# Hash-masked attention with a gated MLP: two outputs written in place, one more buffer in two rings, an odd head's copies three tiles earlier, one small product four tiles later

## The chip, the cores and the metric

The kernel runs on one core of one Trainium2 chip. The metric is the device time of one launch, in microseconds (us). Engines are named as the profile names them: PE is TensorE (matrix products; PEld is its loading of weights), DVE is VectorE, ACT is ScalarE, POOL is GpSimd and SP is SyncE, which only issues DMAs here. A "q" behind an engine (SPq, ACTq) means its instruction queue, where DMAs are issued.

## The reference, cut to what matters

Shapes: batch 4, 8 heads, 768 positions, head dimension 64; model width 512, inner width 1024. Each query and key gets a 6-bit bucket from the signs of its projection, and a query attends only to keys of its own bucket. The attention's output feeds a gated MLP whose gate mixes positions.

```python
q_bits = (einsum('bhsd,dk->bhsk', q, proj) > 0); k_bits = ...
mask = q_bucket[:, :, :, None] == k_bucket[:, :, None, :]
scores = where(mask, matmul(q, k^T) / sqrt(64), -1e9)
attn = exp(scores - max(scores)); attn = attn / (sum(attn) + 1e-9)
x = concat_heads(matmul(attn, v))                      # 4 x 768 x 512
h = maximum(x @ w_in, 0); u, v = h[..., :512], h[..., 512:]
v_n = (v - mean(v)) / sqrt(var(v) + 1e-6)
out = (u * (einsum('ts,bsd->btd', w_spatial, v_n) + b_spatial)) @ w_out
```

## The kernel before, in words

There are 32 heads (4 batches of 8), taken in 16 pairs; `p` or `r` is a pair, `n` a head, `i` one of the six tiles of 128 queries of a head, and `g = 6 n + i` counts tiles. Most values are kept as two fp16 numbers, a high part and a residual, so that fp16 products add up to nearly fp32.

Preparation of a pair: `load_qk` fetches q and k (tile `qk`, one buffer); `hash_rows` makes the signed bits (`sg`); `split_qk` (lines 185 to 191) makes high parts and residuals (`hl`, one buffer), the first on ScalarE (line 188). `build(n)` (lines 193 to 212) copies one head's rows from `hl` and `sg` into one of four operand tiles `ab`, with two large DMAs on SyncE's queue and four small ones, which go on ScalarE's queue for heads from 8 on and on SyncE's before. `split_v` prepares v; `mean_v` (lines 221 to 233) adds v up on GpSimd (lines 225 to 228, the last result is `vc`), sums it over partitions with a product on TensorE (line 230) and copies it into `fm` on ScalarE (line 232). `fm` is for queries whose bucket holds no key, and `normalize` reads it after the head's last tile.

A tile of a query head (`scores`, lines 278 to 301): four products give the masked scores in PSUM (lines 291 and 292); VectorE finds the negated row maximum `nb` (line 293), where the elementwise output `jk` is thrown away; ScalarE takes the exponential into `ex` (line 295, three buffers), copies it to fp16 in `pp` (line 298, `PB` = 3 buffers); VectorE or, for some tiles, GpSimd adds the residual (line 299); a DMA on SyncE's queue transposes `pp` into `pt` (line 301, `PTB` = 5 buffers). `weighted` (lines 303 to 316) multiplies `pt` with v, five tiles later (`LAG`). Heads 1 to 7 (`KEYS`) go another way: scores come out transposed (`scores_k`, lines 256 to 266), the maximum is found ahead (`row_max`), no transpose is needed, and the exponentials lie in the `pt` ring.

When the eight heads of a batch are through, its MLP goes into a queue of 28 units, of which one is taken about every 1.7 tiles: six `v_unit`s (line 361 products, line 365 into `v32m`, four buffers, shared with the output `o` of line 435), which after each third call `norm` (lines 374 to 390): line 388 normalizes into `vy`, line 389 copies it to fp16, line 390 makes the residual on GpSimd; then `u_unit`, `s_unit` and `o_unit`. The last batch's units run by themselves after the last head.

Order: each engine carries out its instructions in a fixed order, made by a planner from priorities (`at(g, k)`, in tiles) and from a simulated timeline. The main loop (lines 504 to 569) sets the priorities. Before, head `n` builds head `n + 2` at its tile 0; the mean of the next pair, its product included, is at tile 5 of the even head; in the odd head v is loaded at tile 1, bits are made at tile 2, `split_qk` comes at tile 3 and `load_qk` at tile 5.

Of the kernel before, what the change touches and what calls it, by code (L numbers as in the profile page):

```python
# [10 lines left out]
BF16 = mybir.dt.bfloat16  # L11
F32 = mybir.dt.float32
# [3 lines left out]
ALU = mybir.AluOpType  # L16
# [3 lines left out]
P = 128  # L20
# [16 lines left out]
def lsh_attention_spatial_gating(  # L37
# [11 lines left out]
    nc = tc.nc  # L49
    B, NPAIR, _, _, S = kq.shape  # L50
    NH = 2 * NPAIR
    NT = S // P
    HS = S // 2
    DM = NPAIR * P
    DF = w_in.shape[1]
    F2 = DF // 2
    NF = F2 // P
    ISQ = 1.0 / (SQ * SQ * 8.0)

    VYB = 2  # L60
    QKB = 1
    PSB = (2,2,2)
    MT = "m"
# [2 lines left out]
    wk = ctx.enter_context(tc.tile_pool(name="wk", bufs=1))  # L66
# [35 lines left out]
    st = {}  # L102
# [65 lines left out]
    def has_queries(p):  # L168
        return not (2 * p in KEYS and 2 * p + 1 in KEYS)
# [23 lines left out]
    def build(n):  # L193
        p, e = divmod(n, 2)
        hl, sg, t = st["hl", p], st["sg", p], ab[n % NAB]
        r = slice(D * e, D * e + D)
        q_s, q_h = (BQ_S[n >= NH], BQ_H[n >= NH])
        if n < 1:
            nc.sync.dma_start(out=t[0:D, 2:4], in_=hl[r, 1:3])
        for j in range(4):  # L200
            q_s.dma_start(
                out=t[D:NR, 3 - j // 2, (j % 2) * HS:(j % 2 + 1) * HS],
                in_=sg[32 * j + 16 * e:32 * j + 16 * e + 2 * NB, :])
        if n < 1:
            q_h.dma_start(out=t[0:D, 0:2], in_=hl[r, 0:2])
        else:

            top = hl[r, 0:2]
            (ps, pn), (ss, sn), (es, en) = top.ap
            src = replace(top, ap=[(ps, pn), (ss, 2), (ss, 2), (es, en)])  # L210
            q_h.dma_start(out=t[0:D].rearrange("p (a b) s -> p a b s", b=2), in_=src)
        q_h.dma_start(out=t[D:P, 0:2], in_=hl[r, 2:4])
# [8 lines left out]
    def mean_v(p):  # L221
        v32 = st["v32", p] if has_queries(p) else vf[p % 2][:, :, 0:D]

        a = wk.tile([P, NT, D], F32, tag="pf", name=f"va{p}")
        nc.gpsimd.tensor_add(a, v32[:, 0:NT], v32[:, NT:2 * NT])
        c = wk.tile([P, 2, D], F32, tag="vc", name=f"vc{p}")
        nc.gpsimd.tensor_add(c, a[:, 0:2], a[:, 2:4])
        nc.gpsimd.tensor_add(c, c, a[:, 4:6])
        mp = ps_m.tile([P, 512], F32, tag=MT, name=f"mp{p}")
        nc.tensor.matmul(mp[:, :P], lhsT=ones, rhs=c.rearrange("p e d -> p (e d)"), start=True, stop=True)  # L230
        fm = wk.tile([P, 2, D], F32, tag="fm", bufs=2, name=f"fm{p}")
        nc.scalar.activation(fm.rearrange("p e d -> p (e d)"), mp[:, :P], AF.Copy, scale=SX / S)
        st["fm", p] = fm
# [44 lines left out]
    def scores(n, i):  # L278
        if n in KEYS:
            scores_k(n, i)  # L280
            return
        t = ab[n % NAB]
        if i == 0:
            st["nb", n] = wk.tile([P, NT], F32, tag="nb", bufs=3, name=f"nb{n}")
        nb = st["nb", n][:, i:i + 1]
        jk = wk.tile([P, 2, HS], BF16, tag="jk", name=f"jk{n}_{i}")
        qs = slice(i * P, (i + 1) * P)
        ps = ps_sc.tile([P, 2, 512], F32, tag="sc", name=f"sp{n}_{i}")[:, :, :HS]
        for c in range(2):
            cs = slice(c * HS, (c + 1) * HS)  # L290
            nc.tensor.matmul(ps[:, c], lhsT=t[:, 0, qs], rhs=t[:, 1, cs], start=True, stop=False)  # L291
            nc.tensor.matmul(ps[:, c], lhsT=t[0:P - 1, 3, qs], rhs=t[0:P - 1, 2, cs], start=False, stop=True)  # L292
        nc.vector.tensor_scalar(jk, ps, -ISQ, None, op0=ALU.mult, op1=ALU.min, accum_out=nb)  # L293
        ex = wk.tile([P, 2, HS], F32, tag="ex", bufs=EB, name=f"ex{n}_{i}")
        st["ex", n, i] = nc.scalar.activation(ex, ps, AF.Exp, bias=nb, scale=ISQ).ins  # L295
        at(NT * n + i + G_H, 50)
        pp = wk.tile([P, 2, 2, HS], F16, tag="pp", bufs=PB, name=f"pp{n}_{i}")
        nc.scalar.copy(pp[:, 0], ex)  # L298
        (nc.gpsimd if i in (PL_POOL if n >= 2 * NH else PL_POOL1) else nc.vector).tensor_tensor(out=pp[:, 1], in0=ex, in1=pp[:, 0], op=ALU.subtract)  # L299
        pt = st["pt", n, i] = wk.tile([P, 2 * NT, P], F16, tag="pt", bufs=PTB, name=f"pt{n}_{i}")  # L300
        st["tr"] = nc.sync.dma_start_transpose(out=pt, in_=pp.rearrange("p g c k -> p (g c k)")).ins
# [48 lines left out]
    def mlp_units(b):  # L350
# [3 lines left out]
        v32 = {}  # L354
# [19 lines left out]
        def norm(g):  # L374
            m = mv[g]
            ve = wk.tile([P, 3], F32, tag="ve", bufs=2, name=f"ve{b}_{g}")
            nc.vector.tensor_scalar(ve, m[:, :, 1], EPS_LN, None, op0=ALU.add)
            r = wk.tile([P, 3], F32, tag="rs", bufs=2, name=f"rs{b}_{g}")
            nc.scalar.activation(r, ve, AF.Ln)
            nc.scalar.activation(r, r, AF.Exp, scale=-0.5)  # L380

            nc.vector.tensor_mul(ve, ve, r)
            nc.vector.scalar_tensor_tensor(out=ve, in0=ve, scalar=-0.5 * SN, in1=r, op0=ALU.mult, op1=ALU.mult)
            nc.vector.scalar_tensor_tensor(out=r, in0=ve, scalar=1.5 * SN, in1=r, op0=ALU.add, op1=ALU.mult)
            for j in range(3):
                i = 3 * g + j
                y = wk.tile([P, F2], F32, tag="vy", bufs=VYB, name=f"vy{b}_{i}")
                nc.vector.tensor_scalar(y, v32[i], m[:, j, 0:1], r[:, j:j + 1], op0=ALU.subtract, op1=ALU.mult)
                nc.scalar.copy(vn[0][:, i], y)
                nc.gpsimd.tensor_tensor(out=vn[1][:, i], in0=y, in1=vn[0][:, i], op=ALU.subtract)  # L390

# [55 lines left out]
    N = B * NH  # L447
    NP = B * NPAIR
# [13 lines left out]
        return 99  # L462

    RB = 3
    PB = 3
    EB = 3
    PTB = 5
    XTB = 6
    LAG = 5
    XL_ENG = nc.vector  # L470
# [9 lines left out]
    BQ_S = (nc.sync, nc.scalar)  # L480
    BQ_H = (nc.sync, nc.sync)
    LQ = nc.sync
    BI = 0

    def at(g, k):
        tc.cur_priority = int(1000 * (g + 40) + k)
# [17 lines left out]
    for g in range(N * NT + LAG):  # L504
        n, i = divmod(g, NT)
        if n < N:
            at(g + G_S, 0)
            scores(n, i)
            r = n // 2
            at(g + G_P, 300)  # L510
            if g == 0:
                hash_rows(1)
                split_qk(1)
                split_v(0)
                load_qk(2)
                load_v(1)
                load_vf(0)
                load_vf(1)
            at(g + G_M, 100)
            while rml and rml[0][0] <= g:  # L520
                row_max(*rml.pop(0)[1:])
            at(g + G_P, 300)
            stack = ExitStack()
            if n not in KEYS:
                stack.enter_context(tc.issue_after(st["tr"]))
            if BQ_S[n + 2 >= NH] is nc.scalar or BQ_H[n + 2 >= NH] is nc.scalar:
                stack.enter_context(tc.issue_after(st["ex", n, i]))
            if i == BI and n + 2 < N:
                build(n + 2)
            if n % 2 == 0:  # L530
                if i == 4 and 0 < r < NP - 1:
                    load_vf(r + 1)
                if i == 5 and r + 1 < NP:
                    split_v(r + 1)
                    mean_v(r + 1)
                if i == 4 and r == 0:
                    mean_v(0)
            else:
                if i == 2 and r + 2 < NP:
                    hash_rows(r + 2)  # L540
                if i == 3 and r + 2 < NP:
                    split_qk(r + 2)
                if i == 5 and r + 3 < NP:
                    load_qk(r + 3)
                if i == 1 and r + 2 < NP:
                    load_v(r + 2)
            stack.close()
        while wv < N * NT and wv + (LAGK if wv // NT in KEYS else LAG) <= g:
            m, j = divmod(wv, NT)
            wv += 1  # L550
            at(g + G_V, 200)
            weighted(m, j)
            if j == NT - 1:
                at(g + G_N, 250)
                normalize(m)
                if m % 2:
                    transpose_x(m // 2)
                    if m % NH == NH - 1:
                        queue += mlp_units(m // NH)
        at(g + G_W, 500)  # L560
        while wdone < W_AT(g):
            wdone += 1
            next(wg, None)
        if queue and n < N:
            credit += 28.0 / DEN
            at(g + G_U, 400)
            while queue and credit >= 1.0:
                queue.pop(0)()
                credit -= 1.0
# [44 lines left out]
```

## Time and profile before

| what | before |
|---|---|
| median of three runs | 738.57 us (736.13 to 741.49) |
| profiled execution, span from first to last instruction | 741.7 us |
| TensorE, VectorE, ScalarE, GpSimd busy | 631.5, 520.6, 434.8, 321.2 us |
| share of the 16 DMA engines, SyncE's queue | 76.4% |
| moved in all | 120.95 MB |

The page gives the span of the profiled execution; a time around the span isn't on it, so the span stands beside the runs' own times. A row of waits reads "who waited <- for whom: us in total, times, longest us". A row of a group reads: line, engine, operation, output <- inputs, shapes, count | busy us, mean ns of one | idle us before, and what ended it. A row of the timeline reads: start us, duration us, engine, line, operation, output <- inputs, count, and in brackets the idle time before it and what ended that. Idle time of an engine that isn't the bound costs nothing.

### The profile page before, as it was taken

The numbers are of one execution on the slowest core, as the hardware profiler recorded it, in microseconds if no ns is written. First come the engines' busy times: TensorE is split into PE (matmuls) and PEld (weight loads), VectorE is DVE, ScalarE is ACT, GpSimd is POOL, SyncE is SP. The second block draws the span as 40 slices with busy tenths as digits, with TensorE's granted clock in tenths as the row PEclk, the third lists the DMA queues.
The fourth block names the chain that finished last, engine by engine and source line by source line (L and its number), as shares of the span: only waits on it lengthen the run. The fifth ranks groups of instructions, "written<-read, shape, count | busy, mean of one in ns | idle before, by whom it ended". The sixth has DMA issues, their size and how long they took to land.

```text
span 741.7 us, 14927 instructions
## 1 busy us (share of the span) xinstructions
PE 631.5 (85%) x5759; PEld 400.4 (54%) x5759; DVE 520.6 (70%) x945; ACT 434.8 (59%) x668; POOL 321.2 (43%) x324
## 2 busy tenths in 40 slices
PE   1569898998988776997898899889898998999997
PEld 0237686776445444554544555556455565654553
DVE  4677795536799999567689798678698987755200
ACT  1344574346788676655676577667677776743221
POOL 5122443123458675264314565156235571451503
PEclk9768797999999989898999999999999999999999
DMA  9565554324999989996999799999999999860011
GB/s 235 149 123 155 133 148 102 99 55 97 224 237 197 215 207 187 213 178 138 234 202 199 138 210 213 211 211 212 206 210 181 194 175 213 182 136 15 1 42 43
DMA packets 290011, 120.95 MB, mean 163 GB/s; under 512 B 270740, under 2 KB 273812, under 8 KB 289940
## 3 DMA queue, kind: packets, MB, share of 16 engines
q1 hardware_dynamic: 287636, 119.11, 76.4%
q10 hardware_dynamic: 2304, 0.89, 0.5%
q8 instruction: 45, 0.74, 0.4%
q14 instruction: 26, 0.21, 0.1%
HBM read 28.33 MB, written 6.29 MB: 47 GB/s over the span
## 4 chain that ended last, share of the span: by engine, by line
PE 43%; DMA 21%; DVE 13%; issue 8%; ACT 6%; POOL 6%; SPq 3%; ACTq 0%; DVEq 0%; POOLq 0%
DMA pt<-pp 14%; PE pv L275 6%; PE vps L361 6%; PE ops L432 5%; PE sps L417 5%; PE ups L402 5%; DMA ab<-hl 4%; PE sp L291 3%; DVE jk L293 3%; PE sp L292 3%; DVE pp L299 2%; PE sp L262 2%; PE pv L314 2%; ACT ex L295 2%; PE sp L263 2%
## 5 line engine op out<-in xcount | busy, mean ns | idle before, releaser
L295 ACT ACTIVATE ex<-sp,nb 128x768 f32<-128x768 f32 x150 | 134.1, 897 | 54.8 <-DVE jk L293 48.9
L299 DVE TENSOR_TENSOR pp<-ex,pp 128x768 f16<-128x768 f32 x116 | 126.2, 1089 | 47.6 <-ACT pp L298 46.5
L293 DVE TENSOR_SCALAR_CACHE_REDUCE jk<-sp 128x768 bf16<-128x768 f32 x150 | 142.4, 949 | 24.1 <-PE sp L292 22.2
L298 ACT CAST pp<-ex 128x768 f16<-128x768 f32 x150 | 124.3, 829 | 50.0 <-DMA pt<-pp 43.9
L314 PE MATMUL pv<-vp,pt 128*128 128x65 f16 x900 | 108.2, 198 | 40.5 <-DMA pt<-pp 40.2
L291 PE MATMUL sp<-ab 128*128 128x384 f16 x300 | 103.2, 344 | 31.6 <-ACT ex L295 19.3
L314 PEld LDWEIGHTS <-pt 128*128 128x128 f16 x900 | 86.7, 101 | 67.2 <-DMA pt<-pp 53.4
L299 POOL TENSOR_TENSOR pp<-ex,pp 128x768 f16<-128x768 f32 x34 | 58.1, 1708 | 131.1 <-ACT pp L298 124.6
L315 PE MATMUL pv<-vp,pt 128*128 128x64 f16 x900 | 108.0, 197 | 0.0
L316 PE MATMUL pv<-vp,pt 128*128 128x65 f16 x900 | 107.8, 198 | 0.0
L292 PE MATMUL sp<-ab 127*128 127x384 f16 x300 | 103.9, 346 | 0.0
L417 PE MATMUL sps<-ws,vn 128*128 128x384 f16 x576 | 100.9, 329 | 1.5 <-DVE sg L180 1.0
L315 PEld LDWEIGHTS <-pt 128*128 128x128 f16 x900 | 87.0, 100 | 11.3 <-issue 1.3
L316 PEld LDWEIGHTS <-pt 128*128 128x128 f16 x900 | 86.9, 100 | 3.1 <-issue 0.5
L417 PEld LDWEIGHTS <-vn 128*128 128x128 f16 x576 | 55.3, 99 | 37.8 <-issue 3.9
L432 PE MATMUL ops<-wo,g 128*128 128x512 f16 x288 | 70.9, 391 | 1.5 <-ACT o L436 0.9
L275 PEld LDWEIGHTS pv<-vf,ex 128*128 128x128 f32 x504 | 68.5, 208 | 4.1 <-issue 1.6
L402 PE MATMUL ups<-xt,wi 128*128 128x384 f16 x384 | 69.1, 333 | 1.3 <-ACT u L405 0.9
L361 PE MATMUL vps<-wi,xt 128*128 128x512 f16 x288 | 68.0, 383 | 1.4 <-DMA xt<-xs 1.3
L275 PE MATMUL pv<-vf,ex 128*128 128x65 f32 x504 | 67.0, 286 | 0.0
L333 POOL TENSOR_TENSOR x<-x,xf 128x384 f32<-128x384 f32 x32 | 35.5, 1110 | 64.1 <-DVE x L332 64.1
L422 POOL TENSOR_TENSOR sy<-sy,u 128x384 f32<-128x384 f32 x32 | 36.6, 1145 | 49.3 <-DVE sy L421 49.2
(87 smaller groups left out, 1010.7 us busy)
## 6 DMA issues: line engine op xcount, KB each, us to landing
qk<-kq SPq DMA_DIRECT2D x16, 768.0 KB
ab<-hl SPq DMA_DIRECT2D x31, 384.0 KB
ab<-hl SPq DMA_DIRECT2D x34, 192.0 KB
out<-o SPq DMA_DIRECT2D x24, 256.0 KB
v<-v SPq DMA_DIRECT2D x13, 384.0 KB
raw<-w_in SPq DMA_DIRECT2D x16, 256.0 KB
pt<-pp SPq DMA_TRANSPOSE x150
raw<-w_sp SPq DMA_DIRECT2D x12, 192.0 KB
```

The source lines that it names most:

```text
L275: nc.tensor.matmul(acc[:, qi, :], lhsT=ex[:, qi * P:(qi + 1) * P], rhs=vf[p % 2][:, 2 * i + e, :], start=(i == 0 and qi == 0), stop=(i == ...
L291: nc.tensor.matmul(ps[:, c], lhsT=t[:, 0, qs], rhs=t[:, 1, cs], start=True, stop=False)
L292: nc.tensor.matmul(ps[:, c], lhsT=t[0:P - 1, 3, qs], rhs=t[0:P - 1, 2, cs], start=False, stop=True)
L293: nc.vector.tensor_scalar(jk, ps, -ISQ, None, op0=ALU.mult, op1=ALU.min, accum_out=nb)
L295: st["ex", n, i] = nc.scalar.activation(ex, ps, AF.Exp, bias=nb, scale=ISQ).ins
L298: nc.scalar.copy(pp[:, 0], ex)
L299: (nc.gpsimd if i in (PL_POOL if n >= 2 * NH else PL_POOL1) else nc.vector).tensor_tensor(out=pp[:, 1], in0=ex, in1=pp[:, 0], op=ALU.subtract)
L314: nc.tensor.matmul(acc, lhsT=pt[:, c, :], rhs=vh, start=(i == 0 and c == 0), stop=False)
L315: nc.tensor.matmul(acc[:, 0:D], lhsT=pt[:, c, :], rhs=vl, start=False, stop=False)
L316: nc.tensor.matmul(acc, lhsT=pt[:, NT + c, :], rhs=vh, start=False, stop=(i == NT - 1 and c == NT - 1))
L361: nc.tensor.matmul(ps, lhsT=xt[c][:, gx, i * P:(i + 1) * P], rhs=wi[gw][:, c, F2:DF], start=(k == 0), stop=(k == 3 * NPAIR - 1))
L417: nc.tensor.matmul(ps[:, :HS], lhsT=vn[gv][:, c, d * P:(d + 1) * P], rhs=ws[gw][:, c, hs], start=(k == 0), stop=(k == 3 * NT - 1))
```

## The change

Five things change. The discarded output `jk` is written into the first half of `ex`, as bf16, and `ex` is therefore taken ahead of line 293. The normalized `y` of `norm` is written over its input `v32[i]`, and the buffers `vy` go. `PB` goes from 3 to 4 and `PTB` from 5 to 6. The even head `n` builds both heads of the next pair, `n + 2` at its tile 0 and `n + 3` at its tile 3, where before the odd head built its own successor `n + 2` at tile 0. The product and the copy of `mean_v` become `mean_mm`, called at tile 3 of the odd head, four tiles after `mean_v` (for pair 0 at tile 0 of head 1).

```diff
-    VYB = 2
...
         nc.gpsimd.tensor_add(c, c, a[:, 4:6])
+        st["vc", p] = c
+
+    def mean_mm(p):
+        c = st.pop(("vc", p))
         mp = ps_m.tile([P, 512], F32, tag=MT, name=f"mp{p}")
         nc.tensor.matmul(mp[:, :P], lhsT=ones, rhs=c.rearrange("p e d -> p (e d)"), start=True, stop=True)
...
-        jk = wk.tile([P, 2, HS], BF16, tag="jk", name=f"jk{n}_{i}")
+        ex = wk.tile([P, 2, HS], F32, tag="ex", bufs=EB, name=f"ex{n}_{i}")
+        jk = ex.rearrange("p c k -> p (c k)").bitcast(BF16)[:, 0:S].rearrange("p (c k) -> p c k", c=2)
...
         nc.vector.tensor_scalar(jk, ps, -ISQ, None, op0=ALU.mult, op1=ALU.min, accum_out=nb)
-        ex = wk.tile([P, 2, HS], F32, tag="ex", bufs=EB, name=f"ex{n}_{i}")
...
-                y = wk.tile([P, F2], F32, tag="vy", bufs=VYB, name=f"vy{b}_{i}")
-                nc.vector.tensor_scalar(y, v32[i], m[:, j, 0:1], r[:, j:j + 1], op0=ALU.subtract, op1=ALU.mult)
+                y = v32[i]
+                nc.vector.tensor_scalar(y, y, m[:, j, 0:1], r[:, j:j + 1], op0=ALU.subtract, op1=ALU.mult)
...
-    PB = 3
+    PB = 4
     EB = 3
-    PTB = 5
+    PTB = 6
...
-    BI = 0
...
-            if i == BI and n + 2 < N:
-                build(n + 2)
+            if n % 2 == 0 and n + 2 < N:
+                if i == 0:
+                    build(n + 2)
+                if i == 3:
+                    build(n + 3)
...
             else:
+                if i == 3 and r + 1 < NP:
+                    mean_mm(r + 1)
+                if i == 0 and r == 0:
+                    mean_mm(0)
```

## The prediction

> **What bounds the kernel now.** I read the page's head first, then the windows that cut the span where the work changes, then the waits and the chain inside the longest window, and at last single tiles in the timeline.
>
> ```profile
> span 741.7 us, 14927 instructions
> PE 631.5 (85%) x5759; PEld 400.4 (54%) x5759; DVE 520.6 (70%) x945; ACT 434.8 (59%) x668; POOL 321.2 (43%) x324
> DMA  9565554324999989996999799999999999860011
> ```
>
> TensorE is busy 85% of the span, but the mean hides four stretches. The windows below have, in order, the length, the busy time of each engine (number of instructions), the granted clock, the DMA share and GB/s.
>
> ```profile
> 0.00:185.40 185.40, 142.39 (x1006) 105.44 (x1007) 116.46 (x218) 85.60 (x135) 60.70 (x85) 0.87 0.53 130
> 185.40:296.70 111.30, 87.83 (x893) 52.57 (x891) 105.12 (x183) 84.81 (x143) 71.01 (x65) 0.93 1.02 211
> 296.70:649.00 352.30, 313.42 (x3297) 194.43 (x3298) 273.68 (x492) 237.93 (x341) 157.48 (x144) 0.96 0.98 196
> 649.00:741.70 92.70, 87.88 (x567) 47.96 (x565) 25.33 (x53) 26.45 (x50) 32.03 (x32) 0.99 0.18 48
> ```
>
> Start (0 to 185, mostly heads 1 to 7): TensorE idles 43.0 us. Second stretch (185 to 297): VectorE is busy 105.12 of 111.30 us, 94%, and is the bound. Third (297 to 649, the long one): TensorE 89%, VectorE 78%, DMA share 0.98, so three resources stand close together; TensorE idles 352.3 - 313.4 = 38.9 us. Tail: TensorE 95% with an idle DMA; nothing in this change shortens it. So what can be won is mostly in the 38.9 us of the third stretch. Its waits (who waited for whom: total us, times, longest):
>
> ```profile
> ACT pp L298 <- DMA pt<-pp: 39.6, 27, 3.7
> PE pv L314 <- DMA pt<-pp: 22.2, 19, 2.9
> ACT hl L188 <- DMA ab<-hl: 10.7, 7, 2.9
> PE sp L291 <- ACT ex L295: 9.3, 8, 5.1
> PE mp L230 <- POOL vc L228: 6.3, 3, 3.7
> ...
> L298 ACT CAST pp<-ex 128x768 f16<-128x768 f32 x108 | 89.5, 830 | 43.6 <-DMA pt<-pp 39.6 <-ACT ex L295 1.3 <-ACT g L423 1.2
> ```
>
> The three TensorE rows make 37.8 of the 38.9 us. The first row is the key: ScalarE's copy into pp waits until the transpose of three tiles before has landed, because pp has three buffers. The chain of the same window says that this is on the path, and how long transposes can take behind other traffic (8.05 us for one, 9.48 us for two in a row):
>
> ```profile
> 477.50 9.48 DMA pt<-pp x2
> 556.68 8.05 DMA pt<-pp
> ```
>
> One turn of the ring, from the timeline around 524 us (start, duration, [idle before]):
>
> ```profile
> 524.12 0.83 ACT L298 CAST pp<-ex 128x768 f16<-128x768 f32 x1 [3.65 <-DMA pt<-pp]
> 524.99 0.96 DVE L299 TENSOR_TENSOR pp<-ex,pp 128x768 f16<-128x768 f32 x1 [4.21 <-ACT pp L298]
> 526.18 1.46 SPq L301 DMA_TRANSPOSE pt<-pp  x1
> ```
>
> ScalarE stands 3.65 us for a buffer, VectorE 4.21 us behind it, and only then is the transpose issued. A turn is copy 0.83, residual 0.96, and transpose 4 to 8 us: 6 to 10 us for three tiles, or 2 to 3.3 us a tile. The stretch does 108 tiles (the last row above, the group of line 298) in 352.3 us, 3.26 us a tile: the ring of three is as slow as the kernel.
>
> **The change, part by part.** Everything below is subtracted from the span of 741.7 us. The runs' median is 738.57 (736.13 to 741.49); the page gives no time around the span, so I take the same 3.1 us off every result.
>
> *PB 3 to 4.* It adds no work; the copy waits for the transpose of four tiles before, one pace (3.26 us) more slack, against waits of at most 3.7 us. So nearly all of ScalarE's 39.6 us can go; that is no gain by itself. The gain for TensorE lies between 0, if the transposes only queue longer on a DMA with share 0.98, and all 22.2 us. I take half, **11.1 us**: waits behind an ordinary transfer go, those behind bursts as in the 8.05 us row stay. Late next are then VectorE at 78% and the DMA.
>
> *PTB 5 to 6.* A transpose needs a free pt buffer. I compared the issue of the 144 transposes of heads 8 to 31 with the last product that read the buffer, five tiles before. The tightest pair is below: the second of these two transposes is issued at 642.2, the last read of its buffer ends at 638.07.
>
> ```profile
> 637.88 0.19 PE L316 MATMUL pv<-vp,pt 128*128 128x65 f16 x1
> 640.69 2.98 SPq L301 DMA_TRANSPOSE pt<-pp  x2
> ```
>
> So five do not bind, and six are worth **0**; if a fourth pp buffer moves transposes a pace forward, the sixth pt keeps it from binding.
>
> *jk into ex.*
>
> ```profile
> L293 DVE TENSOR_SCALAR_CACHE_REDUCE jk<-sp 128x768 bf16<-128x768 f32 x150 | 142.4, 949 | 24.1 <-PE sp L292 22.2
> ```
>
> Line 293's work stays the same (949 ns), and its output lands in the tile that line 295 writes next. The old jk had a single buffer written by VectorE alone and held nobody. Now line 293 of tile k needs ex of tile k-3 free, that is line 299 of k-3 done; behind it on VectorE everything waits, and line 295 and the scores two tiles on wait for it. After 304 us line 293 begins behind that moment in every tile but two (0.1 us each), mostly by 2 to 6 us: hidden. Before, it often runs ahead:
>
> ```profile
> 189.81 0.96 DVE L293 TENSOR_SCALAR_CACHE_REDUCE jk<-sp 128x768 bf16<-128x768 f32 x1 [0.29 <-PE sp L292]
> 190.69 0.95 DVE L299 TENSOR_TENSOR pp<-ex,pp 128x768 f16<-128x768 f32 x1
> ...
> 295.40 0.95 DVE L293 TENSOR_SCALAR_CACHE_REDUCE jk<-sp 128x768 bf16<-128x768 f32 x1
> ...
> 299.43 1.58 DVE L299 TENSOR_TENSOR pp<-ex,pp 128x768 f16<-128x768 f32 x1
> 300.93 0.95 DVE L293 TENSOR_SCALAR_CACHE_REDUCE jk<-sp 128x768 bf16<-128x768 f32 x1
> ```
>
> The pass at 189.81 (tile 13 of the 150) would wait for the residual that ends at 191.64, that at 295.40 (tile 43) for the one that ends at 301.01. Twelve passes, from the first of these rows to the last, lead so, by 22.6 us together, nearly all where VectorE is the bound. Bounds: 0 (the fourth pp makes those residuals a pace earlier, or the two swap places on VectorE without loss) to 22.6 us. I take a loss of **3 us**, nearer to 0: one pace of 3.26 us covers eleven of the leads and leaves 2.3 us of the longest (5.6).
>
> *vy in place.* Line 388 writes into v32m, which the matrix product's output shares; a buffer is held until the GpSimd residual of line 390 instead of line 388.
>
> ```profile
> L389 ACT CAST vn<-vy 128x512 f16<-128x512 f32 x24 | 14.4, 617 | 7.0 <-DVE vy L388 7.0
> L390 POOL TENSOR_TENSOR vn<-vy,vn 128x512 f16<-128x512 f32 x24 | 30.9, 1300 | 40.7 <-ACT vn L389 40.7
> DVE vy L388 <- POOL vn L390: 2.6, 2, 1.9
> ```
>
> It removes VectorE's 2.6 us for vy, and holds a buffer 617 + 1300 ns longer. The fifth and sixth unit of each of four batches could meet that: at most 8 x 1.9 = 15 us of ScalarE. In the tail a unit lasts 15.54 / 6 = 2.59 us on TensorE, and the second PSUM buffer covers one unit: **0**, between +2.6 and -15.
>
> ```profile
> 666.62 15.54 PE vps L361 x72
> ```
>
> *Odd head's copies at tile 3 of the even head.*
>
> ```profile
> ab<-hl SPq DMA_DIRECT2D x31, 384.0 KB
> ab<-hl SPq DMA_DIRECT2D x34, 192.0 KB
> ab<-sg ACTq DMA_DIRECT2D x96, 9.0 KB
> ```
>
> Nothing is added: per head two copies from hl on SyncE's queue and four small ones from sg, on ScalarE's queue from head 8 on. They move three tiles forward, past three transposes, which now land behind 576 KB at even tile 3 and no longer at odd tile 0, just ahead of the v load of odd tile 1. The target ab buffer was last read by the head before: free. What goes is ScalarE's wait at line 188 for hl, since six tiles instead of three pass before it:
>
> ```profile
> ACT hl L188 <- DMA ab<-hl: 20.4, 11, 3.9
> 338.87 1.48 ACT L188 ACTIVATE hl<-qk 128x1536 f16<-128x1536 f32 x1 [2.87 <-DMA ab<-hl]
> 344.56 0.90 ACT L295 ACTIVATE ex<-sp,nb 128x768 f32<-128x768 f32 x1 [3.08 <-DVE jk L293]
> ```
>
> After that 2.87 us stall the exponential of 344.56 came late, and TensorE lost its longest 5.1 us (the 9.3 us row). Bounds 0 to 9.3; I take **3 us**, and **2 us** for the first stretch, an estimate: part of the 20.4 us and some of the mean's waits lie there, in a TensorE that idles 43 us mostly for other things.
>
> *Mean's matmul four tiles later.* TensorE, in order, waits for GpSimd's three sums (line 228 last). Four tiles are 13 us of cover. The normalization that reads fm comes more than ten tiles later still. Removed: 6.3 us in the third stretch; I take **4.3**, as the next product in the queue won't always be ready.
>
> Sum: -11.1 + 3 - 3 - 2 - 4.3 = -17.4; 741.7 - 17.4 - 3.1 = **721 us**.
>
> A rule against the largest term: the Trainium skill, Perfetto Trace Analysis, What "DMA-bound" means, says that a kernel can be bound by the issuing engine's sequencer when its track is solid with DMA slices.
>
> ```profile
> L301 SPq DMA_TRANSPOSE pt<-pp x150: 1277/1605/3941, 28.7 to 655.7; - x150
> ```
>
> At the median, 108 transposes take 173 us of SyncE in 352: about half, not solid, so by that page too it isn't yet the bound; by its rule the first term would be 0 if it were.
>
> **The rivals.**
> *The DMA is the bound and the wait only moves* (0.22). For it: share 0.98, and issues stretched to 3941 ns. Against: TensorE's waits come singly, 19 in 108 tiles. The first term goes: -17.4 + 11.1 = -6.3, **732 us**.
> *All stalls go and the clock comes back* (0.13). 22.2 + 6.3 + 4.7 (half of 9.3) + 2 - 3 = 32.2 us; and the granted clock of 0.96 over 352.3 us is 14 us of lost clock, a third of which, 5 us, may return with fewer gaps: **701 us**. Against: VectorE would need 273.7 us in some 320, 86%. The Trainium skill, TensorE: Matmul & The Clock Gate, HAM oscillation, says idle gaps beyond about 3.4 us halve the clock; here the gaps are mostly shorter, so it gives less.
> *VectorE is held by ex: slower* (0.14). If the residuals of the second stretch don't come earlier, its 22.6 us are paid at the bound, and with the DMA full the first term fails as well: +22.6 - 4.3 - 3 - 2 = +13.3, **752 us**. It decides where line 293 leads line 299 by more than three tiles.
> *The planner undoes it* (0.06). Instructions are ordered by priority and planned time; the new order may spend what the buffers save: **739 us**.
>
> **How the numbers follow.** Forecast 721 (712 to 731): 0.45. A measurement tells about 1% from no change, so faster is below 731.2, slower above 746. Faster: 0.43 of the forecast, 0.13, and 0.06 of the DMA case: 0.62. Slower: 0.12 of the ex case and 0.01 of the planner: 0.13. The rest, 0.25, same. The range 706 to 745 leaves out two thirds of the clock case (0.09) and most of the ex case (0.11).
>
> **What would show it.** Right: line 298's wait for pt<-pp falls from 39.6 us in the third stretch to under 12, line 314's from 22.2 to about 11, line 230's and 188's to near 0, TensorE above 92% there. Wrong: line 314's wait unchanged with longer transposes (DMA), or line 293 waiting for line 299 or an idle VectorE between 185 and 297 (ex), or line 365 waiting for line 390 (vy).

## The result, and the profile after

The changed kernel's median is 734.2 us (20 runs), against 738.33 us of 20 runs of the kernel before on the same chip: ratio 0.9937, interval 0.991 to 0.9965. The ratio goes by the undisturbed runs alone, so it isn't quite the quotient of the medians. That is 0.6%, some 4.6 us, where 17 were forecast. The profiled execution after spans 731.0 us (device time 732.79), 10.7 less than that of before. That is more than the ratio of the many runs says, so the profiles show where, not how much.

The page's head after, then the four windows, cut where the DMA's load changes as before (columns as before: length, busy time of PE, PEld, DVE, ACT and POOL with counts, granted clock, DMA share, GB/s):

```profile
span 731.0 us, 14930 instructions
PE 628.9 (86%) x5759; PEld 395.9 (54%) x5759; DVE 520.3 (71%) x945; ACT 432.0 (59%) x668; POOL 323.2 (44%) x324
```

```profile
0.00:181.40 181.40, 138.41 (x1013) 101.34 (x1014) 114.55 (x218) 83.54 (x133) 58.25 (x84) 0.92 0.52 132
181.40:289.60 108.20, 84.77 (x811) 50.38 (x811) 93.87 (x163) 79.04 (x135) 67.09 (x61) 0.88 1.02 209
289.60:638.60 349.00, 317.99 (x3376) 196.47 (x3374) 288.28 (x513) 243.45 (x352) 165.52 (x148) 0.97 1.02 201
638.60:731.00 92.40, 87.69 (x565) 47.67 (x563) 23.59 (x53) 25.98 (x50) 32.37 (x32) 1.00 0.17 48
```

The third stretch, where nearly all was to be won, still has TensorE busy only 91% and idle 31.0 us (38.9 before). The counts of instructions differ a little from before, so the windows don't hold quite the same work. Cut at the last product with v of tiles 6, 43 and 149, the two executions compare piece by piece: the first part is 2.8 us shorter, tiles 6 to 43 4.0 (140.0 to 136.0), tiles 43 to 149 3.5 (337.1 to 333.6), the tail 0.4.

```profile
183.50:323.50 140.00, 114.91 (x1134) 69.28 (x1135) 121.14 (x209) 102.79 (x170) 82.76 (x76) 0.91 1.01 210
323.50:660.60 337.10, 299.40 (x3216) 186.61 (x3216) 266.90 (x483) 226.67 (x325) 156.09 (x142) 0.97 0.97 193
```

```profile
180.70:316.70 136.00, 109.08 (x1074) 65.29 (x1071) 119.03 (x209) 100.00 (x165) 79.40 (x73) 0.87 1.01 205
316.70:650.30 333.60, 306.07 (x3272) 189.81 (x3271) 272.06 (x483) 227.71 (x329) 162.39 (x145) 0.98 1.01 199
```

(First before, then after.) Now the waits inside the third stretch after, and one row of the same view of before:

```profile
ACT ex L298 <- DVE ex L297: 51.9, 44, 3.9
...
PE pv L317 <- DMA pt<-pp: 23.2, 20, 4.3
...
ACT pp L301 <- DMA pt<-pp: 8.8, 7, 3.5
...
PE sp L295 <- ACT ex L298: 3.1, 6, 0.9
```

```profile
ACT ex L295 <- DVE jk L293: 26.6, 25, 3.1
```

(Lines 293, 295, 298, 299, 301 and 314 of before are 297, 298, 301, 302, 304 and 317 after.) This is the centre of the result. ScalarE's wait for a pp buffer fell from 39.6 to 8.8 us, as forecast. TensorE's wait for the transposed tile did not: 22.2 before, 23.2 after. And ScalarE took up the wait at another place: for VectorE's row maximum, 26.6 to 51.9 us. What TensorE did lose of its idle time here lies in the two smaller rows: its wait for ScalarE's exponential fell from 9.3 to 3.1 us, and that for `vc`, 6.3 us before, is gone.

Two places in the timeline show how. The first is VectorE and GpSimd at the start of the second stretch (start, duration, what ended the idle time):

```profile
184.81 0.96 DVE L297 TENSOR_SCALAR_CACHE_REDUCE ex<-sp 128x768 bf16<-128x768 f32 x1 [1.65 <-POOL pp L302]
```

```profile
183.14 1.64 POOL L302 TENSOR_TENSOR pp<-ex,pp 128x768 f16<-128x768 f32 x1 [2.83 <-ACT pp L301]
```

The row maximum of tile 12 stands 1.65 us until GpSimd's residual of tile 9 has read the `ex` buffer: the wait that the shared tile added. In the second place a residual of tile 58 runs on VectorE, and SyncE's queue follows behind it:

```profile
360.79 0.96 DVE L302 TENSOR_TENSOR pp<-ex,pp 128x768 f16<-128x768 f32 x1 [0.75 <-ACT pp L301]
```

```profile
361.57 1.99 SPq L304 DMA_TRANSPOSE pt<-pp  x1
363.66 0.53 SPq L440 DMA_DIRECT2D out<-o  x1
364.29 1.75 SPq L304 DMA_TRANSPOSE pt<-pp  x1
366.10 0.84 SPq L210 DMA_DIRECT2D ab<-hl  x1
366.99 0.59 SPq L211 DMA_DIRECT2D ab<-hl  x1
367.69 5.15 SPq L304 DMA_TRANSPOSE pt<-pp  x2
```

```profile
373.64 0.20 PE L317 MATMUL pv<-vp,pt 128*128 128x65 f16 x1 [0.69 <-DMA pt<-pp]
```

The residual ends at 361.75; its transpose is the first of the two issued at 367.69, six microseconds later, because SyncE issues in order behind two other transposes, an output and the odd head's copies. TensorE, which waits for it, goes on at 373.64. Here a tile that is ready earlier only stands longer in this queue.

### The profile page after: what moved, and what is told of

Read it like the earlier page. It is cut to its first block, busy times and chain, and to the rows that moved or that the text cites. A ratio compares the mean times of both kernels' runs of the same rounds, so it can differ in the third digit from the quotient of the medians.

```text
span 731.0 us, 14930 instructions
## 1 busy us (share of the span) xinstructions
PE 628.9 (86%) x5759; PEld 395.9 (54%) x5759; DVE 520.3 (71%) x945; ACT 432.0 (59%) x668; POOL 323.2 (44%) x324
## 5 line engine op out<-in xcount | busy, mean ns | idle before, releaser
L297 DVE TENSOR_SCALAR_CACHE_REDUCE ex<-sp 128x768 bf16<-128x768 f32 x150 | 141.3, 949 | 34.0 <-PE sp L296 31.1
L302 DVE TENSOR_TENSOR pp<-ex,pp 128x768 f16<-128x768 f32 x116 | 127.8, 1109 | 32.1 <-ACT pp L301 31.7
L317 PE MATMUL pv<-vp,pt 128*128 128x65 f16 x900 | 108.7, 198 | 39.9 <-DMA pt<-pp 39.5
L301 ACT CAST pp<-ex 128x768 f16<-128x768 f32 x150 | 123.2, 830 | 16.5 <-DMA pt<-pp 10.9
L295 PE MATMUL sp<-ab 128*128 128x384 f16 x300 | 103.1, 344 | 26.4 <-ACT ex L298 15.8
L420 PE MATMUL sps<-ws,vn 128*128 128x384 f16 x576 | 104.3, 337 | 2.2 <-DVE sy L424 2.1
L278 PEld LDWEIGHTS pv<-vf,ex 128*128 128x128 f32 x504 | 65.8, 201 | 4.4 <-issue 1.9
L364 PE MATMUL vps<-wi,xt 128*128 128x512 f16 x288 | 66.5, 381 | 1.8 <-DMA xt<-xs 0.8
L405 PE MATMUL ups<-xt,wi 128*128 128x384 f16 x384 | 66.8, 326 | 0.0
L278 PE MATMUL pv<-vf,ex 128*128 128x65 f32 x504 | 64.8, 279 | 0.0
L336 POOL TENSOR_TENSOR x<-x,xf 128x384 f32<-128x384 f32 x32 | 37.5, 1171 | 51.1 <-DVE x L335 51.1
L425 POOL TENSOR_TENSOR sy<-sy,u 128x384 f32<-128x384 f32 x32 | 39.2, 1224 | 42.8 <-DVE sy L424 42.6
```

What stands on the lines that cost most here:

```text
L278: nc.tensor.matmul(acc[:, qi, :], lhsT=ex[:, qi * P:(qi + 1) * P], rhs=vf[p % 2][:, 2 * i + e, :], start=(i == 0 and qi == 0), stop=(i == ...
L317: nc.tensor.matmul(acc, lhsT=pt[:, c, :], rhs=vh, start=(i == 0 and c == 0), stop=False)
L420: nc.tensor.matmul(ps[:, :HS], lhsT=vn[gv][:, c, d * P:(d + 1) * P], rhs=ws[gw][:, c, hs], start=(k == 0), stop=(k == 3 * NT - 1))
```

## The experiments

Each ratio is to the kernel before, from runs of both on one chip, with its 95% interval. An edit is to the changed kernel unless another is named. Most rows rest on 10 to 12 runs, u4, e1 and e5 on six, e2 and e7 on four.

| run | ratio | interval |
|---|---|---|
| u1: three pp buffers again | 0.9994 | 0.9967 to 1.0021 |
| u2: copies at the odd head's tile 0 again | 0.994 | 0.991 to 0.997 |
| u3: mean's product at its old place | 0.9977 | 0.9948 to 1.0007 |
| u4: `jk` in a tile of its own | 0.9878 | 0.9843 to 0.9914 |
| u5: `vy` in tiles of its own | 1.0015 | 0.9976 to 1.0054 |
| e1: four `ex` buffers | 0.9869 | 0.981 to 0.9927 |
| e2: 14 loads of q and k left out | 0.9822 | 0.9744 to 0.99 |
| e3: the same in the kernel before | 0.9972 | 0.9933 to 1.001 |
| e4: 32 residuals more on GpSimd | 0.999 | 0.9959 to 1.002 |
| e5: four `ex`, three pp buffers | 1.0112 | 1.0076 to 1.0149 |
| e6: before with the two in-place edits alone | 0.9943 | 0.9908 to 0.9978 |
| e7: a third of most MLP products left out | 0.9769 | 0.9712 to 0.9826 |
| s1, s3: after, other order (credit 0.3, 0.6) | 1.0094, 1.0067 | 1.0062 to 1.0126, 1.0037 to 1.0098 |
| s2, s4: before, other order (0.3, 0.6) | 1.003, 1.0006 | 0.9996 to 1.0063, 0.9974 to 1.0039 |
| s5, s6: e1, other order (0.3, 0.6) | 0.9953, 1.0023 | 0.9912 to 0.9994, 0.9994 to 1.0052 |

**Undoing the parts one by one.** u1, three pp buffers:

```diff
-    PB = 4
+    PB = 3
```

> The changed kernel with pp at three buffers again, all else kept. Theory A (the wait at the pp buffer only moved to VectorE's order and SyncE's queue, so the fourth buffer brings little): 734 to 737 us, at most 3 us slower than the changed kernel, with line 301's wait for the transpose back near 40 us and the exponential's wait for line 297 back below 70 us. Theory B (the fourth buffer brings the gain and another part of the change loses it again): 740 to 748 us. Theory C (the planner's new order decides, whatever the buffer): anywhere within 1% without the waits explaining it.

Measured: 0.9994, so 0.6% is lost again. Its waits over the whole span, and below them those of after and of before:

```profile
ACT ex L298 <- DVE ex L297: 62.6, 48, 5.3
...
ACT pp L301 <- DMA pt<-pp: 47.2, 31, 3.7
PE pv L317 <- DMA pt<-pp: 36.4, 32, 4.0
```

```profile
ACT ex L298 <- DVE ex L297: 90.0, 66, 5.3
...
PE pv L317 <- DMA pt<-pp: 39.5, 31, 4.3
...
PE sp L295 <- ACT ex L298: 15.8, 17, 2.7
...
ACT pp L301 <- DMA pt<-pp: 10.9, 9, 3.5
```

```profile
ACT ex L295 <- DVE jk L293: 48.9, 38, 5.0
...
ACT pp L298 <- DMA pt<-pp: 43.9, 33, 3.7
...
PE pv L314 <- DMA pt<-pp: 40.2, 32, 4.0
```

The fourth buffer takes ScalarE's wait (47.2 to 10.9) and adds one for the row maximum (62.6 to 90.0). TensorE's wait is no smaller with it: 36.4 with three, 39.5 with four. u2, the copies where they were:

```diff
-            if n % 2 == 0 and n + 2 < N:
-                if i == 0:
-                    build(n + 2)
-                if i == 3:
-                    build(n + 3)
+            if i == 0 and n + 2 < N:
+                build(n + 2)
```

> The changed kernel with the odd head's copies back at its predecessor's tile 0 of the odd head. Prediction's term: 3 us of the third stretch and part of 2 us before it, so 737 to 739 us, with line 187's wait for the hl copies back from 7 to about 20 us. Rival (the copies' place only shifts which transposes wait): 733 to 735 us.

Measured: 0.994, the same as after. ScalarE's wait for `hl` (line 187, 188 before) comes back by half (7.4 us after, 14.9 here, 20.4 before), and no time goes with it.

```profile
ACT hl L187 <- DMA ab<-hl: 14.9, 8, 3.9
```

u3, the mean's product behind its sums:

```diff
                     mean_v(r + 1)
+                    mean_mm(r + 1)
...
-                if i == 3 and r + 1 < NP:
-                    mean_mm(r + 1)
```

> The changed kernel with the mean's product back in tile 5 of the even head. Prediction's term: 4.3 us of the third stretch and up to 3.9 us in the start, so 737 to 741 us, with TensorE waiting 8 to 12 us for GpSimd's sums. Rival (TensorE then waits less elsewhere, since transposes land later than its queue asks for them): 733 to 736 us although that wait is back.

Measured: 0.9977, 0.4% or 3 us behind after, of the size of the forecast's 4.3; but the wait itself is 3.9 us in all here, and the intervals overlap.

u4, `jk` apart from `ex` (with five pt buffers, for room; the changed kernel planned with five or with six has the same order on every engine):

```diff
-        jk = ex.rearrange("p c k -> p (c k)").bitcast(BF16)[:, 0:S].rearrange("p (c k) -> p c k", c=2)
+        jk = wk.tile([P, 2, HS], BF16, tag="jk", name=f"jk{n}_{i}")
...
-    PTB = 6
+    PTB = 5
```

> The changed kernel with jk in a buffer of its own again (ex then taken behind line 297 as before) and five pt buffers, which the prediction put at nothing. If taking ex ahead of the row maximum holds VectorE: 726 to 731 us, with the wait of the exponential for line 297 (90 us now) falling by 15 us or more. If it is hidden, as the prediction had it but for 3 us: 731 to 735 us. If the sixth pt buffer carries the gain: 737 us or more.

Measured: 0.9878, 0.6% better than after. The gain lies where the forecast put the loss: from tile 6 to tile 43, u4's profiled execution takes 128.2 us against 136.0 after. The row maximum runs ahead of the residual of three tiles before in 14 of 141 tiles here, in as many before the change, and in none after. u5, the normalized `y` in its own tiles:

```diff
-                y = v32[i]
-                nc.vector.tensor_scalar(y, y, m[:, j, 0:1], r[:, j:j + 1], op0=ALU.subtract, op1=ALU.mult)
+                y = wk.tile([P, F2], F32, tag="vy", bufs=2, name=f"vy{b}_{i}")
+                nc.vector.tensor_scalar(y, v32[i], m[:, j, 0:1], r[:, j:j + 1], op0=ALU.subtract, op1=ALU.mult)
...
-    PTB = 6
+    PTB = 5
```

> The changed kernel with the two vy buffers back and five pt buffers; jk stays in ex. Prediction's term for vy in place: 0, so 733 to 736 us. If holding v32m until line 393 costs: 727 to 732 us, with line 368 no longer waiting for line 393.

Measured: 1.0015, 0.8% worse than after, from an edit on which no wait of size hangs. Such a result is no worth of that edit; it made me doubt all single comparisons, and the runs s1 to s6 come from it.

**Which resource paces the transposes.** e2 and e3 leave transfers out, in the kernel after and before: from the third pair on, the second pair's q and k are used again.

```diff
+        if p >= 2:
+            st["qk", p] = st["qk", p - 1]
+            return
```

> The changed kernel with q and k fetched for the first two pairs only; later pairs use the second pair's, so 14 transfers of 768 KB are left out and their results are wrong values of the same shape. At some 4.3 us each it takes 60 us from the DMA queue. Theory DMA-bound (the wait only moved to the transposes' queue): 690 to 710 us, with line 317's wait for transposes falling from 39.5 to below 25 us. Rival VectorE- or TensorE-bound: 722 to 734 us.

> The kernel before with the same 14 fetches of q and k left out. If the fourth pp buffer was wasted on a full DMA queue, this gains less than the changed kernel does by the same edit, since its ring of three still holds it: 715 to 728 us, and the distance between the two grows from 0.6% to 2% or more. If the distance stays at about 0.6%, the DMA is not where the fourth buffer's gain went.

Measured: 0.9822 and 0.9972. Without the loads the change is worth 1.5% instead of 0.6%, and the 14 loads are worth 1.2% after and 0.3% before. So transfers may hold back some of the gain; but 1.2% is no more than a new order alone makes (below), and TensorE's wait for transposes is not relieved, 42.5 us here against 39.5 (e2's line numbers are three higher):

```profile
ACT ex L301 <- DVE ex L300: 89.2, 64, 5.3
...
PE pv L320 <- DMA pt<-pp: 42.5, 30, 3.9
```

e4 takes work from VectorE:

```diff
-    PL_POOL = (2,)
+    PL_POOL = (0, 2, 4)
```

> The changed kernel with three residuals of line 302 in six on GpSimd in place of one, for heads 16 to 31: 32 residuals of 1.1 us (35 us) leave VectorE, at 1.7 us each (56 us) on GpSimd. Theory VectorE-bound: 718 to 728 us. Rival DMA- or TensorE-bound: 732 to 738 us, or longer where GpSimd's later residuals delay the transposes.

Measured: 0.999, 0.5% worse than after. VectorE's busy time fell from 520.3 to 499.6 us and bought nothing in this order:

```profile
PE 623.0 (85%) x5759; PEld 394.5 (54%) x5759; DVE 499.6 (68%) x913; ACT 432.3 (59%) x668; POOL 370.0 (50%) x356
```

e7 takes work from TensorE:

```diff
+        TWO = THREE if b == B - 1 else THREE[:2]
...
-                for gx, gw in THREE:
+                for gx, gw in TWO:
...
-                for gw, gx in THREE:
+                for gw, gx in TWO:
...
-                    for gg, gw in THREE:
+                    for gg, gw in TWO:
```

> The changed kernel without the third product of the first, second and last matrix products of the MLP for batches 0 to 2 (the residual of the left factor is left out there): at full speed 24 x 216 + 32 x 162 + 24 x 216 ns = 15.6 us a batch, 47 us of TensorE in all, none of it in the tail. If TensorE's own work paces the stretch: 690 to 700 us, most of the 47 us. If VectorE or the DMA pace it: 720 to 732 us, with TensorE's idle time up by 35 us or more.

Measured: 0.9769. The 240 products left out (5759 less 5519) take some 47 us at 0.2 us each; 1.7% against after, 12 to 15 us, came off. In the profiled execution TensorE's busy time is 35.0 us less, at a granted clock of 0.930 against 0.949 after. Its idle time, span less busy, grew from 102.1 to 127.6 us, and its wait for transposes to 56.4:

```profile
PE 593.9 (82%) x5519; PEld 378.8 (52%) x5519; DVE 525.5 (73%) x945; ACT 431.8 (60%) x668; POOL 328.1 (45%) x324
```

```profile
PE pv L317 <- DMA pt<-pp: 56.4, 44, 4.3
```

So, as far as one order of each can tell, none of the three is the one bound; with any one relieved, the rest of the loop takes most of it back.

**The parts in other combinations.** e1 gives `ex` a fourth buffer, so that the row maximum waits for the residual of four tiles before, not three; its ratio is the lowest of the kernels that leave nothing out, level with u4's:

```diff
-    EB = 3
-    PTB = 6
+    EB = 4
+    PTB = 5
```

> The changed kernel with four ex buffers in place of three and five pt buffers in place of six; jk still in ex. Theory ex-ring (line 297 of a tile held until the residual of three tiles before; giving jk its own buffer took 90 to 64 us off the exponential's wait and 0.6% off the time): 728 to 732 us, like jk in its own buffer, and line 297 no longer right behind line 302 of three tiles before. Rival (what helped was another order by the planner, or the place of the buffers): 733 to 736 us.

Measured: 0.9869 (726.25 us against 737.64), 0.7% better than after. Tiles 6 to 43 take 126.80 us, with VectorE busy 92% of it against 88% after (119.03 of 136.00 above). The granted clock there was 0.93 against 0.87, so a part of this could be the clock's; the pairs below speak against it.

```profile
179.40:306.20 126.80, 95.89 (x1033) 57.95 (x1032) 116.39 (x207) 98.01 (x162) 79.14 (x70) 0.93 1.10 215
```

e5 is e1 with three pp buffers (its edit against after: `PB = 3`, `EB = 4`, `PTB = 5`).

> The changed kernel with four ex buffers (which gave 0.987 of the time before) but three pp buffers, and five pt. It tells what the fourth pp buffer is worth once the ex ring doesn't hold the row maximum. Theory: the ex ring ate part of it, so here the missing pp buffer costs 8 to 12 us: 734 to 738 us. Rival: the fourth pp buffer is worth the same 4 us with and without: 730 to 732 us.

Measured: 1.0112, 2.4% worse than e1. Here TensorE's wait does move with the buffers, 51.1 us against 34.3 in e1:

```profile
ACT pp L301 <- DMA pt<-pp: 52.0, 31, 3.6
PE pv L317 <- DMA pt<-pp: 51.1, 40, 4.0
```

```profile
PE pv L317 <- DMA pt<-pp: 34.3, 31, 3.1
```

e6 is the kernel before with only these two edits (`ex` is taken ahead of `jk`, as in the change):

```diff
-        jk = wk.tile([P, 2, HS], BF16, tag="jk", name=f"jk{n}_{i}")
+        jk = ex.rearrange("p c k -> p (c k)").bitcast(BF16)[:, 0:S].rearrange("p (c k) -> p c k", c=2)
...
-                y = wk.tile([P, F2], F32, tag="vy", bufs=VYB, name=f"vy{b}_{i}")
+                y = v32[i]
```

> The kernel before with the two in-place outputs alone; three pp and five pt buffers, the odd head's copies and the mean's product where they were. Theory ex-ring: its price shows here without any gain, 742 to 748 us, and the price lies in the stretch between 185 and 325 us. Rival: with three pp buffers the residuals and the row maximum are held alike anyway, so 736 to 741 us.

Measured: 0.9943, as fast as the whole change, with three pp buffers, the full wait for them, and two edits that were to cost or to be worth nothing:

```profile
ACT pp L301 <- DMA pt<-pp: 46.3, 30, 4.1
...
PE pv L317 <- DMA pt<-pp: 35.2, 35, 3.7
```

The parts contradict each other: undone one at a time, pp is worth 0.6, the mean 0.4 and `vy` 0.8%, and `jk` costs 0.6; yet e6, without pp, copies and mean, has the whole gain.

**The order by itself.** Every edit above also makes the planner order the instructions anew, which shows in SyncE's queue even between u1 and after. So the last six runs change nothing but the order. The MLP's units are taken off their queue by a credit that grows each tile; starting it at 0.3 or 0.6 of a unit takes each unit about half a tile or one tile sooner, with the same instructions and buffers.

```diff
-    credit = 0.0
+    credit = 0.3
```

(s3, s4 and s6 have 0.6.) The kernel after and the kernel before:

> The changed kernel with the MLP's credit starting at 0.3 in place of 0: its units come half a tile earlier, no work, buffer or transfer is changed, and the planner makes another order. Planner theory (an order is worth several us by chance): 725 to 742 us, off the changed kernel's 0.994 by 0.4% or more. Part theory (the differences are the parts' own): 0.992 to 0.996 of the kernel before, 731 to 735 us.

> The kernel before with the MLP's credit starting at 0.3. Planner theory: 728 to 748 us, off the kernel before by 0.4% or more. Part theory: within 0.3% of it.

> The changed kernel with the credit starting at 0.6, a whole tile earlier: a third order of the same program. Planner theory: the three orders of the changed kernel spread over 0.5 to 1.5%. Part theory: within 0.3% of the changed kernel.

> The kernel before with the credit starting at 0.6. Planner theory: the three orders of the kernel before spread over 0.5 to 1.5%, and the means of the two sets of three differ by less than their spread. Part theory: within 0.3% of the kernel before.

and e1:

> Four ex and five pt buffers, the changed kernel otherwise, with the MLP's credit starting at 0.3. If the ex ring is a mechanism, it lies as far below the changed kernel with the same shift (1.009) as without (0.987 against 0.994) or further: 0.99 to 1.002, 730 to 739 us. If 0.987 was the order's luck: 1.004 to 1.015, 740 to 748 us.

> The same with the credit starting at 0.6. Mechanism: 0.988 to 1.0 against the changed kernel's 1.007, 728 to 737 us. Luck: 1.002 to 1.012, 739 to 746 us.

Measured, with the original order first: before 1, 1.003, 1.0006; after 0.9937, 1.0094, 1.0067; e1 0.9869, 0.9953, 1.0023. Order alone moves the kernel after by 1.6% and e1 by 1.5%, and the kernel before by 0.3%. Set side by side, the change moves the time by -0.6, +0.6 and +0.6%: no gain over these three orders (mean 1.0033 after, 1.0012 before). In s1, 1.6% slower than after, the three waits followed so far are like those of after; a fourth is not:

```profile
ACT ex L298 <- DVE ex L297: 96.8, 70, 5.3
PE pv L317 <- DMA pt<-pp: 35.5, 26, 3.7
PE sp L295 <- ACT ex L298: 27.8, 22, 4.7
...
ACT pp L301 <- DMA pt<-pp: 7.0, 4, 2.4
```

The pp wait is gone in it as well, and TensorE's wait for transposes is even 4 us shorter: neither says how fast the kernel is. What grew is TensorE's wait for ScalarE's exponential, from 15.8 to 27.8 us, about as much as the span grew between these two executions (731.0 to 741.9). The fourth `ex` buffer, on the other hand, gains in all three orders, 0.7, 1.4 and 0.4%, 0.84% or 6 us on average, though the intervals of the first and the last pair overlap. The profiles put it where it is expected: tiles 6 to 43 take 136.0 us after and 126.8 in e1, 138.5 in s1 and 125.7 in s5 (the granted clock is 0.90 in both), 135.7 in s3 and 130.7 in s6. TensorE's wait for the exponential is shorter with it in each pair (14.4, 16.7 and 13.8 us against 15.8, 27.8 and 20.8).

## Why the prediction was wrong, step by step

The size came out wrong: 734.2 us lies in the range of 706 to 745, but at 0.6% and not at the 17 us of the sum. The direction came out right by the luck of one order: with two other orders the changed kernel is the slower one.

*PB, -11.1: the step that failed.* The wait on the pp buffer fell as foretold (39.6 to 8.8 us in the third stretch; under 12 was asked). That half of TensorE's own wait would go with it was the error: that wait went from 22.2 to 23.2 and not to 11. Over the whole span it is 35 to 51 us in six profiles with three buffers (before, u1, e3, e5, e6, s4; mean 40) and 34 to 56 in the thirteen with four (mean 44). Buffers that come free sooner let ScalarE copy sooner, but the tile then waits elsewhere: over tiles 44 to 145, in the means of before and after, the step from residual to issue of the transpose grew from 0.89 to 1.54 us and that from copy to residual from 1.30 to 1.76, while issue to landing stayed (4.63 and 4.57) and the tile lay landed 1.75 us instead of 2.28. From row maximum to last product it is 15.22 before and 15.31 after; as the products come five tiles behind the scores in TensorE's order, this sum follows the pace (3.25 and 3.18 us a tile) and says nothing by itself. So the first rival's outcome came, the wait that only moves, but not by its reason: landings are no longer, and e2 has no shorter wait. The tile stands in two queues of fixed order, VectorE's and SyncE's. SyncE's queue is fuller than the forecast read it: 108 transposes at the median of the row below (min/median/max in ns) come to 162 us of 349, but the longer ones and the other issues count too. Added up row by row, SyncE issues for 264.5 us of the third stretch, 76% (260.7 of 352.3 before, 74%, where the forecast had 173 us and about half).

```profile
L304 SPq DMA_TRANSPOSE pt<-pp x150: 1278/1504/4168, 28.7 to 645.7; - x150
```

By the rule that was weighed, the Trainium skill, Perfetto Trace Analysis, What "DMA-bound" means, three quarters are still not the solid track that would make the sequencer the bound. But a queue that is a quarter idle on average can be solid for a while, as from 361.57 to 367.69 above, and there it held the tile. No run gave SyncE less to issue and nothing else, so how much of TensorE's wait is this queue's stays open. What the fourth buffer is worth in time stays unsettled too: u1 and e5 speak for 0.6 and 2.4%, e6 against any.

*jk into ex, +3: right mechanism, too small.* A fourth `ex` buffer gives 0.84%, 6 us, in the mean of three orders; `jk` apart gives 0.6% (one order). It lies in the second stretch, where the forecast had it: 136.0 us after, 126.8 in e1. The sign named for it, an idle VectorE, shows beside e1 (17.0 us idle after between tiles 6 and 43, 10.4 there) but not beside before (18.9). The discount failed, that a fourth pp buffer would bring the residuals a pace forward and cover eleven of twelve leads. In the second stretch before, ScalarE hardly waited for pp, so there was little to bring forward:

```profile
ACT pp L298 <- DMA pt<-pp: 4.3, 6, 2.0
```

What the late residuals waited for instead was not counted. (The twelve leads add up to 23.8 us in the trace, a little over the 22.6 of the forecast.)

*PTB, 0, and vy, 0.* PTB was not tried alone on the chip; that the planned order is the same with five fits the 0. Line 368 (365 before) waits for line 393 (390) in the third stretch for 1.9 us in all, which fits the 0 of vy too; the 0.8% of u5 is no more than an order makes.

*The odd head's copies, -3, and 2 for the first stretch.* The wait for `hl` went from 20.4 to 7.4 us, and in u2 giving half of it back cost nothing (0.994 and 0.9937), as if ScalarE had slack there. The first stretch did come out 4 us shorter, but in one execution of each; up to tile 6 it is 183.5 us before and 183.3 in s4, against 180.7, 182.0 and 183.8 in after, s1 and s3, so nothing is shown.

*The mean, -4.3.* TensorE's wait for `vc`, 10.6 us over the span before, is gone; u3 makes it 3 us, inside what orders make. Neither confirmed nor refuted.

*The planner, 0.06: far too little weight.* This rival was priced at giving back 17 us with a chance of 6%. In the runs an order alone makes 1.6% for the same instructions and buffers, more than the whole change. The other two orders of the kernel after are 0.6% slower than before with the same credit, so even the sign of a small change depends on it. The forecast read its terms off the waits of one planned order; these waits move with the order.

*All stalls go, 0.13.* They did not: TensorE still idles 31.0 us in the third stretch. The granted clock there was 0.96 before and 0.97 after, in one execution of each.

Two things stay open. Why TensorE waits 34 to 56 us for transposes whatever is relieved: a likely reason is that the planned order puts a product where the planner expected its tile, so that any lateness shows and any earliness doesn't; no run shows it. And which feature of an order makes 1.6%: in s1 the loss sits in TensorE's wait for the exponential, but what in the order made that wait is not known.

## What to carry to other kernels

A wait that vanishes is worth only what the bound engine's own wait loses; look up the two in the same window, and if work between them runs in fixed queues, expect the wait to move along. How full a queue is must be added up from all its issues, not from a median. Before an output is put into a ring that is read later, count how far its writer runs ahead of that ring, and give the ring one buffer more (here 6 us). Where a planner makes the order, shift something harmless and time three orders of both kernels before trusting a difference under 2%.

## What the runs showed of the hardware beyond that

SyncE holds back a transpose whose data is ready: it stood 6 us behind two transposes that took 1.99 and 1.75 us to issue and three other transfers (361.75 to 367.69 above). And the time that one such issue takes is uneven: 1278 ns at the least, 1504 at the median and 4168 at the most for the same 128x1536 tile, so a median times a count falls short of what the queue is busy.
